# Attention pairs 2 and 3 are transposed by the DMA engine, and the later pairs follow another plan

## The chip, the cores and the metric

The kernel runs on one core of a Trainium2 chip. The metric is device time in microseconds (us) of one execution, taken as the median of several runs. The engines are TensorE (PE in the rows, with PEld for its weight loads), VectorE (DVE), ScalarE (ACT), GpSimd (POOL) and SyncE (SP), which here only issues DMAs. Each works through its own list of instructions in order, and waits on the others through semaphores.

## The reference

```python
def _attn_ref(q, k, v):                       # 8 batches, 8 heads, 576 tokens, 64 per head
    q_c = q.reshape(B, H, nc, chunk, D)       # chunk = 64; k_c and v_c alike
    scores = scale * np.matmul(q_c, k_c.transpose(0, 1, 2, 4, 3))
    scores = scores - np.max(scores, axis=-1, keepdims=True)
    attn = np.exp(scores)
    attn = attn / (np.sum(attn, axis=-1, keepdims=True) + 1e-09)
    return np.matmul(attn, v_c)

def _moe_ref(x, w_in, w_out):                 # x is 4608 x 512, d_ff is 2048
    h = x @ w_in
    sp = np.where(h > 20.0, h, np.log1p(np.exp(np.minimum(h, 20.0))))
    return ((h * np.tanh(sp)) @ w_out).astype(np.float32)
```

The output of the attention, with heads side by side, is the x of the second function.

## The kernel before

The 4608 tokens are 36 tiles of 128, taken as 18 pairs numbered 0 to 17. For each pair the attention goes through the same steps: scores on PE, maximum, subtraction, exponential on ScalarE, sums, reciprocal and normalisation on VectorE, a transposition of the normalised p, and then the values on PE (av), which end in x. The feed-forward part needs x.

**First part.** Pairs 0 to 3 feed two plain blocks of 16 slots each. In slot s PE does `up(s+1)` (12 matmuls into h), then any attention of the slot, then `down(s-1)` (12 matmuls into o_o). `down(i)` begins with g_lo(i), which VectorE makes at line 411 after ScalarE's g_hi(i). In the first block the fp32 weights are also prepared on the fly: SP loads a piece into `sums` (line 163), ScalarE does `scale` and `hi`, VectorE `bits` (lines 192 and 193) and `lo` (line 211). The table `softmax` says in which slot each step of pairs 2 and 3 stands. There the transposition is 8 PE matmuls with an identity (`a_transpose`, line 332) and a ScalarE copy out of PSUM (`a_copy`, line 342).

**Second part.** From then on a list of steps, about 1.2 us of PE each, alternates matmuls into al, b and g (line 881) with matmuls into d (line 1000). `MEET` gives the step at which each of the pairs 8 to 17 begins and ends; a pair of 14 steps uses the plan `NEAR`, one below 30 steps `MID`, a longer one `FAR`. Pairs of 28 steps or more already go through the DMA: for each half t of a pair GpSimd's `p_split` (line 787) parts the 16-bit halves of the words, `p_turn` (line 793, on SP) transposes them by DMA, and GpSimd's `p_join` (line 799) puts the words together again. The two halves share one spare room, so the second half runs seven steps behind. All other pairs are transposed by PE (line 770). Loads of q and k stand 9 steps ahead of a pair's start.

Every load and store but a few at the start is issued by SP, in the order of the program: an instruction there that waits holds back all that stand behind it.

Of the kernel before, what the change touches and what calls it, by code (L numbers as in the profile page):

```python
# [9 lines left out]
F32 = mybir.dt.float32  # L10
# [3 lines left out]
U16 = mybir.dt.uint16  # L14
# [4 lines left out]
P = 128  # L19
CHUNK = 64  # L20
# [5 lines left out]
def kernel(  # L26
# [65 lines left out]
    def view(name, start, shape, dtype=F32):  # L92

        n = math.prod(shape)
        o = rooms[name]
        assert start % 4 == 0 and start // 4 + n <= o.shape[1]
        o = o[:, start // 4 : start // 4 + n]
        if dtype != F32:
            o = o.bitcast(dtype)
        if len(shape) > 1:  # L100
            names = "abcde"[: len(shape)]
            o = o.rearrange(
                f"p ({' '.join(names)}) -> p {' '.join(names)}", **dict(zip(names, shape))
            )
        return o
# [232 lines left out]
    def a_copy(j, t=BOTH):  # L338
        d = st[j]
        if t.start == 0:  # L340
            d["ps"] = at.tile([P, 2, H, CHUNK], F32, name=f"ps_{j}", tag="A")
        nc.scalar.copy(
            out=d["ps"][:, t].rearrange("p t h k -> p (t h k)"),
            in_=d["pt", t.start][:, : t.stop - t.start].rearrange("p t g n -> p (t g n)"),
        )

    def a_values(j, t=BOTH, place=HOME):
        small_mm(banks(j, "av", t, place), st[j]["v"], st[j]["ps"], t)
# [431 lines left out]
            in_=d["pt"][:, t].rearrange("p g n -> p (g n)"),  # L780
        )

    def half_words(slot):
        return view("c", 2 * KB * slot, [DM]).bitcast(U16)

    def p_split(j, t):
        nc.gpsimd.tensor_copy(
            out=half_words((2, 0)[t]).rearrange("p (b n) -> p b n", b=2),
            in_=half_words(t).rearrange("p (n b) -> p b n", b=2),
        )  # L790

    def p_turn(j, t):
        nc.sync.dma_start_transpose(
            out=half_words(t).rearrange("p (m n) -> p m n", n=P), in_=half_words((2, 0)[t])
        )

    def p_join(j, t):
        st[j]["p", t] = view("c", 2 * KB * (2, 0)[t], [NG, 2, CHUNK])
        nc.gpsimd.tensor_copy(
            out=half_words((2, 0)[t]).rearrange("p (n b) -> p b n", b=2),  # L800
            in_=half_words(t).rearrange("p (b n) -> p b n", b=2),
        )

# [234 lines left out]
    def s_store(b, half, js):  # L1038
# [16 lines left out]
        "exp": {7: (2, 3)},  # L1055
        "sum": {7: (2,), 8: (3,)},
        "norm": {8: (2,), 9: (3,)},
        "t": {9: (2,), 12: (3,)},
        "v": {10: (2,), 13: (3,)},
    }  # L1060

    AHEAD = list(range(FIRST_TILE // 2, FIRST_TILE // 2 + 4))
# [19 lines left out]
    def slot(s):  # L1082
# [6 lines left out]
            up(s + 1, last="w")  # L1089
        if "v" in e:  # L1090
            a_values(e["v"])
        for j in a["t"]:
            a_transpose(j)
        for j in a["v"]:
            a_values(j)
        if 1 <= s < N - 1:
            down(s - 1)
        for j in a["s"]:
# [30 lines left out]
            a_transpose(e["norm"])  # L1129
        for j in a["norm"]:  # L1130
            a_norm(j)
        for j in a["t"]:
            a_copy(j)
        if s < NF and a["exp"]:
            g_hi(s)
            g_lo(s)
# [26 lines left out]
            a_copy(e["norm"])  # L1163
        for j in a["v32"]:
            load_v(j)
        later = quick.get(s + 1, {})
        if "load" in later and s > NF:
            e_load(later["load"], "k")
# [57 lines left out]
        for k, m in (2, 0), (5, 3), (3, 4), (4, 7):  # L1226
            when(z, m, lambda k=k: x_sum(b, k))

    MEET = (36, 50, 64, 92, 148, 162, 190, 204, 260, 288, 307)
    NEAR = dict(exp=5, sum=(6, 7), norm=(7, 8), t=11)  # L1230
    MID = dict(exp=5, sum=(8, 9), norm=(10, 12), t=16)
    FAR = dict(exp=33, sum=(36, 37), norm=(38, 40), t=44)
    pe = {}

    def plan_pair(j, start, end):

        n = NEAR if end - start < 16 else MID if end - start < 30 else FAR

        def at_(m, *ops):
            when(*divmod(m, STEPS), *ops)  # L1240

        def on_pe(m, op):
            pe.setdefault(divmod(m, STEPS), []).append(op)

        at_(8 if start == MEET[0] else start - 9, lambda: p_load(j))
        on_pe(start, lambda: p_scores(j, start // STEPS))
        at_(start + 3, lambda: load_v(j))
        for t in range(2):
            at_(start + 1 + 2 * t, lambda t=t: p_max(j, t))
            at_(start + 2 + 2 * t, lambda t=t: p_sub(j, t))  # L1250
            at_(start + n["exp"], lambda t=t: p_exp(j, t))
            at_(start + n["sum"][t], lambda t=t: p_sum(j, t))
            at_(start + n["norm"][t], lambda t=t: p_norm(j, t))
            if end - start < 28:
                at_(start + n["t"] + 1, lambda t=t: p_copy(j, t))
            else:
                m = start + n["norm"][0] + 7 * t
                at_(m + 1, lambda t=t: p_split(j, t))
                at_(m + 2, lambda t=t: p_turn(j, t))
                at_(m + 8, lambda t=t: p_join(j, t))  # L1260
            at_(end + 1, lambda t=t: a_x(j, t))
        if end - start < 28:
            on_pe(start + n["t"], lambda: p_transpose(j))
        on_pe(end, lambda: p_values(j))

# [19 lines left out]

    with tc.manual_schedule():
        prologue()
        x1_open()
        for s in range(N - 1):
            slot(s)  # L1290
            if s == N - 5:
# [32 lines left out]
        ps_b = ctx.enter_context(tc.tile_pool(name="ps_b", bufs=1, space=bass.MemoryType.PSUM))  # L1324
        for n in "b", "g":
            places[n] = ps_b.tile([P, DM], F32, name=n, tag=n)
        for j, pair in zip(range(AHEAD[-1] + 1, NPAIR), zip(MEET, MEET[1:])):
            plan_pair(j, *pair)
        for m, step in (5, t_sum), (6, t_diff), (21, t_hi), (23, t_lo):
            when(*divmod(m, STEPS), lambda step=step: step(*LAST_JOB))  # L1330
        for z in 3, 17:
# [52 lines left out]
```

## Time and profile before

| | before |
|---|---|
| median of 3 runs | 795.29 us (794.58 to 795.43) |
| the profiled execution | 795.96 us, of which 794.1 us is the span of its instructions |
| PE busy | 781.3 us, 98% of the span |
| DVE, ACT, POOL busy | 592.6, 475.9 and 296.1 us |
| granted TensorE clock | 0.999 on average |
| DMA | 204.95 MB, 258 GB/s |

The span runs from the first to the last instruction. "Busy" counts instructions that are running, so PE's 98% leaves some 13 us in which it stands still, half of them at the end.

### The profile page before, as it was taken

The page shows a single profiled execution, that of the slowest core. Times are in us where ns is not written, and L with a number is a line of the kernel's source. Part 1 is how long each engine was busy: PE and PEld are TensorE (multiplying, and loading weights), DVE is VectorE, ACT ScalarE, POOL GpSimd, SP SyncE. Part 2 cuts the span into 40 slices and gives each one's busy share as a digit, 9 for nine tenths or more (in the row PEclk, how much of TensorE's full clock was granted, in tenths as well). Part 3 has the DMA queues.
Part 4 walks back from the last instruction along what each step waited for, and adds up shares of the span by engine and source line. Part 5 has one row for each costly group of instructions (what it writes and reads, how often), then busy time and mean ns, then how long its engine had stood idle before and what let it go on. Part 6 is the DMA issues. An engine that isn't in the chain of part 4 may idle for free.

```text
span 794.1 us, 15299 instructions
## 1 busy us (share of the span) xinstructions
PE 781.3 (98%) x5940; PEld 701.4 (88%) x5940; DVE 592.6 (75%) x929; ACT 475.9 (60%) x855; POOL 296.1 (37%) x259
## 2 busy tenths in 40 slices
PE   8999999999999999999999999999999999999996
PEld 7887888888889999999899999999999999999986
DVE  6897978888866776799577679977575897455666
ACT  5988865666676665555566466647465654644440
POOL 2000026556363235533434435454433452333340
PEclk9999999999999999999999999999999999999999
DMA  7798867989978777765987866689965667866537
GB/s 292 245 312 292 276 229 242 350 285 333 374 244 295 268 263 222 291 225 181 328 333 237 297 254 233 220 234 373 284 235 185 227 217 242 291 224 220 182 117 172
DMA packets 95112, 204.95 MB, mean 258 GB/s; under 512 B 24128, under 2 KB 47168, under 8 KB 87872
## 3 DMA queue, kind: packets, MB, share of 16 engines
q1 hardware_dynamic: 90752, 202.01, 74.9%
q10 hardware_dynamic: 4288, 1.97, 1.0%
q8 instruction: 47, 0.77, 0.4%
q14 instruction: 25, 0.20, 0.1%
HBM read 162.53 MB, written 38.80 MB: 254 GB/s over the span
## 4 chain that ended last, share of the span: by engine, by line
PE 75%; DVE 10%; ACT 6%; DMA 3%; issue 2%; POOL 1%; SPq 0%; DVEq 0%; POOLq 0%; ACTq 0%
PE d L1000 28%; PE al L881 16%; PE o_o L424 8%; PE g L881 8%; PE h L389 7%; PE b L881 4%; DMA k<-in_k 2%; PE av L256 2%; DVE sums L1028 1%; DVE sums L1031 1%; PE al L720 1%; DMA v<-in_v 1%; DVE c L192 1%; PE s L256 1%; DVE c L760 1%
## 5 line engine op out<-in xcount | busy, mean ns | idle before, releaser
L1000 PE MATMUL d<-u,wo 128*128 128x448 f32 x796 | 203.8, 363 | 0.0
L1028 DVE TENSOR_TENSOR sums<-d,sums 128x448 f32<-128x448 f32 x192 | 118.8, 619 | 78.4 <-PE d L1000 78.1
L881 PE MATMUL al<-xo,ring 128*128 128x448 f32 x768 | 174.6, 362 | 0.0
L1000 PEld LDWEIGHTS d<-u,wo 128*128 128x128 f32 x796 | 148.6, 187 | 11.7 <-DVE u L960 0.6
L881 PEld LDWEIGHTS al<-xo,ring 128*128 128x128 f32 x768 | 143.3, 187 | 11.0 <-ACT sums L926 0.5
L881 PE MATMUL g<-xo,ring 128*128 128x448 f32 x384 | 87.6, 363 | 0.2 <-ACT y L926 0.2
L881 PEld LDWEIGHTS g<-xo,ring 128*128 128x128 f32 x384 | 71.6, 187 | 5.4 <-ACT y L926 0.6
L1000 PE MATMUL d<-yr,wo 128*128 128x448 f32 x192 | 56.7, 363 | 0.0
L1000 PE MATMUL d<-xo,wo 128*128 128x448 f32 x182 | 54.9, 364 | 0.0
L1000 PE MATMUL d<-g,wo 128*128 128x448 f32 x174 | 51.9, 363 | 0.2 <-DVE sums L1028 0.2
L950 ACT ACTIVATE b<-b 128x448 f32<-128x448 f32 x32 | 16.9, 528 | 52.0 <-DVE b L936 51.9
L640 POOL TENSOR_TENSOR c<-c 128x256 f32<-128x256 f32 x12 | 10.8, 901 | 98.2 <-DVE c L608 96.2
L881 PE MATMUL b<-xo,ring 128*128 128x448 f32 x192 | 43.6, 362 | 0.0
L950 ACT ACTIVATE y<-y 128x448 f32<-128x448 f32 x22 | 12.7, 577 | 47.6 <-DVE y L936 47.6
L982 POOL TENSOR_TENSOR z<-y,z 128x448 f32<-128x448 f32 x24 | 27.8, 1157 | 35.8 <-DVE y L982 21.9
L424 PE MATMUL o_o<-xo,g 128*128 128x512 f32 x168 | 40.8, 392 | 0.1
L389 PE MATMUL h<-x,xo 128*128 128x512 f32 x168 | 40.9, 392 | 0.0
L950 ACT ACTIVATE z<-g 128x448 f32<-128x448 f32 x32 | 17.4, 544 | 39.0 <-DVE g L936 28.0
L1000 PEld LDWEIGHTS d<-yr,wo 128*128 128x128 f32 x192 | 36.0, 187 | 2.7 <-ACT sums L1026 0.3
L881 PEld LDWEIGHTS b<-xo,ring 128*128 128x128 f32 x192 | 36.0, 187 | 2.5
L424 PEld LDWEIGHTS o_o<-xo,g 128*128 128x128 f32 x168 | 31.2, 188 | 6.6 <-DVE g L411 0.2
L389 PEld LDWEIGHTS h<-x,xo 128*128 128x128 f32 x168 | 31.2, 188 | 6.5
(261 smaller groups left out, 1656.3 us busy)
## 6 DMA issues: line engine op xcount, KB each, us to landing
ring<-dwi SPq DMA_DIRECT2D x56, 1024.0 KB, 7.1
wo<-dwo SPq DMA_DIRECT2D x112, 512.0 KB, 4.5
sums<-in_w_in SPq DMA_DIRECT2D x16, 512.0 KB, 5.4
sums<-in_w_out SPq DMA_DIRECT2D x16, 512.0 KB, 5.6
q<-in_q SPq DMA_DIRECT2D x16, 512.0 KB, 6.4
k<-in_k SPq DMA_DIRECT2D x16, 512.0 KB, 6.9
v<-in_v SPq DMA_DIRECT2D x16, 512.0 KB, 6.3
dwo<-sums SPq DMA_DIRECT2D x15, 512.0 KB, 5.2
```

What stands on the lines that cost most here:

```text
L192: nc.vector.scalar_tensor_tensor(out=c, in0=c, scalar=3, in1=a[:, :, 0], op0=left, op1=either)
L256: nc.tensor.matmul(o[h * CHUNK : (h + 1) * CHUNK, c, t - ts.start, g], lhsT=l[rows, t, 2 * g + h], rhs=r[rows, t, 2 * g + h], start=True, ...
L389: nc.tensor.matmul(h[:, cols], lhsT=wi(f, w_, kt), rhs=x[:, kt, cols], start=(n == 0), stop=(n == 3 * NK - 1),)
L424: nc.tensor.matmul(acc[t], lhsT=g[:, sl], rhs=w_part(f, w_), start=(f == 0 and n == 0), stop=(f == NF - 1 and n == 2),)
L640: nc.gpsimd.tensor_tensor(out=o, in0=a, in1=b, op=op)
L720: nc.tensor.matmul(d["s", c][h * CHUNK : (h + 1) * CHUNK, t, g], lhsT=d["q"][rows, t, 2 * g + h], rhs=d["k"][rows, t, 2 * g + h], start=Tr ...
L760: nc.vector.tensor_tensor(out=p, in0=p, in1=r.unsqueeze(3).broadcast_to([P, 2, NG, CHUNK]), op=ALU.mult)
L881: nc.tensor.matmul(o[:, :HALF], lhsT=w_[:, wn, kt * P : (kt + 1) * P], rhs=x[:, xn, kt], start=(n == 0 and k < 3), stop=(n == 5), skip_gro ...
L950: nc.scalar.activation(out=take(z, 12) if n == 12 else i, in_=i, func=AF.Mish)
L982: engine.tensor_tensor(out=o, in0=l, in1=r, op=ALU.subtract)
L1000: nc.tensor.matmul(o[:, :HALF], lhsT=wos[(len(DOWN) * y + kk) % 4][:, i, part, h * P : (h + 1) * P], rhs=x, start=(m == 0 and k in (5, 2, 1)),
L1028: nc.vector.tensor_tensor(out=o, in0=i, in1=o, op=ALU.add)
```

## The change

Pairs 2 and 3 no longer use PE and ScalarE for the transposition. GpSimd splits, SP issues the DMA transposes, GpSimd joins (`a_split`, `a_turn`, `a_join`), with the room `early` as the spare place for pair 2 and a fresh buffer for pair 3; `x1` is therefore opened later. The values of pair 2 stand in slot 11 where they were in slot 10. In the second part the two halves get separate spare rooms (the second one at the end of `x32`), the second half's split stands 2 steps behind the first's, each join 10 steps behind its normalisation, loads have a list of their own (`LOAD`), and pair 17 ends at step 316 and so goes through the DMA as well.

```diff
--- before.py
+++ after.py
@@ -343,6 +343,35 @@
             out=d["ps"][:, t].rearrange("p t h k -> p (t h k)"),
             in_=d["pt", t.start][:, : t.stop - t.start].rearrange("p t g n -> p (t g n)"),
         )
+
+    def words(x, t):
+        return x[:, t].bitcast(U16)
+
+    def a_split(j, x):
+        d = st[j]
+        d["x"] = x
+        d["w"] = d["p"].rearrange("p t g c k -> p t (g c k)")
+        for t in range(2):
+            nc.gpsimd.tensor_copy(
+                out=words(x, t).rearrange("p (b n) -> p b n", b=2),
+                in_=words(d["w"], t).rearrange("p (n b) -> p b n", b=2),
+            )
+
+    def a_turn(j):
+        d = st[j]
+        for t in range(2):
+            nc.sync.dma_start_transpose(
+                out=words(d["w"], t).rearrange("p (m n) -> p m n", n=P), in_=words(d["x"], t)
+            )
+
+    def a_join(j):
+        d = st[j]
+        for t in range(2):
+            nc.gpsimd.tensor_copy(
+                out=words(d["x"], t).rearrange("p (n b) -> p b n", b=2),
+                in_=words(d["w"], t).rearrange("p (b n) -> p b n", b=2),
+            )
+        d["ps"] = d["x"].rearrange("p t (h k) -> p t h k", k=CHUNK)
 
     def a_values(j, t=BOTH, place=HOME):
         small_mm(banks(j, "av", t, place), st[j]["v"], st[j]["ps"], t)
@@ -780,24 +809,27 @@
             in_=d["pt"][:, t].rearrange("p g n -> p (g n)"),
         )
 
-    def half_words(slot):
-        return view("c", 2 * KB * slot, [DM]).bitcast(U16)
+    def p_place(n):
+        return ("c", 2 * KB * n) if n < 3 else ("x32", 14 * KB)
+
+    def half_words(n):
+        return view(*p_place(n), [DM]).bitcast(U16)
 
     def p_split(j, t):
         nc.gpsimd.tensor_copy(
-            out=half_words((2, 0)[t]).rearrange("p (b n) -> p b n", b=2),
+            out=half_words(t + 2).rearrange("p (b n) -> p b n", b=2),
             in_=half_words(t).rearrange("p (n b) -> p b n", b=2),
         )
 
     def p_turn(j, t):
         nc.sync.dma_start_transpose(
-            out=half_words(t).rearrange("p (m n) -> p m n", n=P), in_=half_words((2, 0)[t])
+            out=half_words(t).rearrange("p (m n) -> p m n", n=P), in_=half_words(t + 2)
         )
 
     def p_join(j, t):
-        st[j]["p", t] = view("c", 2 * KB * (2, 0)[t], [NG, 2, CHUNK])
+        st[j]["p", t] = view(*p_place(t + 2), [NG, 2, CHUNK])
         nc.gpsimd.tensor_copy(
-            out=half_words((2, 0)[t]).rearrange("p (n b) -> p b n", b=2),
+            out=half_words(t + 2).rearrange("p (n b) -> p b n", b=2),
             in_=half_words(t).rearrange("p (b n) -> p b n", b=2),
         )
 
@@ -1055,8 +1087,10 @@
         "exp": {7: (2, 3)},
         "sum": {7: (2,), 8: (3,)},
         "norm": {8: (2,), 9: (3,)},
-        "t": {9: (2,), 12: (3,)},
-        "v": {10: (2,), 13: (3,)},
+        "split": {8: (2,), 9: (3,)},
+        "turn": {8: (2,), 10: (3,)},
+        "join": {9: (2,), 11: (3,)},
+        "v": {11: (2,), 13: (3,)},
     }
 
     AHEAD = list(range(FIRST_TILE // 2, FIRST_TILE // 2 + 4))
@@ -1089,10 +1123,10 @@
             up(s + 1, last="w")
         if "v" in e:
             a_values(e["v"])
-        for j in a["t"]:
-            a_transpose(j)
         for j in a["v"]:
             a_values(j)
+            if j == 2:
+                x1_open()
         if 1 <= s < N - 1:
             down(s - 1)
         for j in a["s"]:
@@ -1129,8 +1163,13 @@
             a_transpose(e["norm"])
         for j in a["norm"]:
             a_norm(j)
-        for j in a["t"]:
-            a_copy(j)
+        for j in a["join"]:
+            a_join(j)
+        for j in a["split"]:
+            if j == 2:
+                a_split(j, view("early", 0, [2, DM]))
+            else:
+                a_split(j, at.tile([P, 2, DM], F32, name=f"x_{j}", tag="A"))
         if s < NF and a["exp"]:
             g_hi(s)
             g_lo(s)
@@ -1163,6 +1202,8 @@
             a_copy(e["norm"])
         for j in a["v32"]:
             load_v(j)
+        for j in a["turn"]:
+            a_turn(j)
         later = quick.get(s + 1, {})
         if "load" in later and s > NF:
             e_load(later["load"], "k")
@@ -1226,13 +1267,14 @@
         for k, m in (2, 0), (5, 3), (3, 4), (4, 7):
             when(z, m, lambda k=k: x_sum(b, k))
 
-    MEET = (36, 50, 64, 92, 148, 162, 190, 204, 260, 288, 307)
+    MEET = (36, 50, 64, 92, 148, 162, 190, 204, 260, 288, 316)
+    LOAD = (8, 38, 52, 80, 118, 150, 178, 192, 230, 276)
     NEAR = dict(exp=5, sum=(6, 7), norm=(7, 8), t=11)
-    MID = dict(exp=5, sum=(8, 9), norm=(10, 12), t=16)
-    FAR = dict(exp=33, sum=(36, 37), norm=(38, 40), t=44)
+    MID = dict(exp=5, sum=(8, 9), norm=(10, 12))
+    FAR = dict(exp=33, sum=(36, 37), norm=(38, 40))
     pe = {}
 
-    def plan_pair(j, start, end):
+    def plan_pair(j, load, start, end):
 
         n = NEAR if end - start < 16 else MID if end - start < 30 else FAR
 
@@ -1242,7 +1284,7 @@
         def on_pe(m, op):
             pe.setdefault(divmod(m, STEPS), []).append(op)
 
-        at_(8 if start == MEET[0] else start - 9, lambda: p_load(j))
+        at_(load, lambda: p_load(j))
         on_pe(start, lambda: p_scores(j, start // STEPS))
         at_(start + 3, lambda: load_v(j))
         for t in range(2):
@@ -1251,15 +1293,15 @@
             at_(start + n["exp"], lambda t=t: p_exp(j, t))
             at_(start + n["sum"][t], lambda t=t: p_sum(j, t))
             at_(start + n["norm"][t], lambda t=t: p_norm(j, t))
-            if end - start < 28:
+            if n is NEAR:
                 at_(start + n["t"] + 1, lambda t=t: p_copy(j, t))
             else:
-                m = start + n["norm"][0] + 7 * t
+                m = start + n["norm"][t]
                 at_(m + 1, lambda t=t: p_split(j, t))
                 at_(m + 2, lambda t=t: p_turn(j, t))
-                at_(m + 8, lambda t=t: p_join(j, t))
+                at_(m + 10, lambda t=t: p_join(j, t))
             at_(end + 1, lambda t=t: a_x(j, t))
-        if end - start < 28:
+        if n is NEAR:
             on_pe(start + n["t"], lambda: p_transpose(j))
         on_pe(end, lambda: p_values(j))
 
@@ -1285,7 +1327,6 @@
 
     with tc.manual_schedule():
         prologue()
-        x1_open()
         for s in range(N - 1):
             slot(s)
             if s == N - 5:
@@ -1324,8 +1365,8 @@
         ps_b = ctx.enter_context(tc.tile_pool(name="ps_b", bufs=1, space=bass.MemoryType.PSUM))
         for n in "b", "g":
             places[n] = ps_b.tile([P, DM], F32, name=n, tag=n)
-        for j, pair in zip(range(AHEAD[-1] + 1, NPAIR), zip(MEET, MEET[1:])):
-            plan_pair(j, *pair)
+        for j, steps in zip(range(AHEAD[-1] + 1, NPAIR), zip(LOAD, MEET, MEET[1:])):
+            plan_pair(j, *steps)
         for m, step in (5, t_sum), (6, t_diff), (21, t_hi), (23, t_lo):
             when(*divmod(m, STEPS), lambda step=step: step(*LAST_JOB))
         for z in 3, 17:
```

On PE, the first block from slot 9 on, before the change. Here h is `up`, o_o is `down`, pt the transposition and av the values:

```order
L389 MATMUL h_920<-x_89,xo 128x512 x12
L332 MATMUL pt_0_933<-ident,p_643 128x128 x8
L424 MATMUL o_o_489<-xo,g 128x512 x6
L424 MATMUL o_o_490<-xo,g 128x512 x6
L389 MATMUL h_977<-x_89,xo 128x512 x12
L256 MATMUL av_0_990<-ps_962,v_814 64x64 x32
L424 MATMUL o_o_489<-xo,g 128x512 x6
L424 MATMUL o_o_490<-xo,g 128x512 x6
L389 MATMUL h_1056<-x_89,u 128x512 x12
```

The same slots with the change:

```order
L418 MATMUL h_919<-x_89,xo 128x512 x12
L453 MATMUL o_o_484<-xo,g 128x512 x6
L453 MATMUL o_o_485<-xo,g 128x512 x6
L418 MATMUL h_970<-x_89,xo 128x512 x12
L453 MATMUL o_o_484<-xo,g 128x512 x6
L453 MATMUL o_o_485<-xo,g 128x512 x6
L418 MATMUL h_1016<-x_89,u 128x512 x12
L256 MATMUL av_0_1029<-early,v_809 64x64 x32
```

The eight transposes are gone from slot 9, and the values of pair 2 have moved behind the `up` of slot 11.

On GpSimd, the end of the start-up and what follows it (p_638 is the p of pair 2, p_807 that of pair 3, L669 is line 640 of before, the first work on the second block's weights):

```order
L211 TENSOR_TENSOR ring<-c,ring 128x512 x2
L355 COPY early<-p_638 128x1024 x2
L370 COPY early<-p_638 128x2x512 x2
L355 COPY x_954<-p_807 128x1024 x2
L370 COPY x_954<-p_807 128x2x512 x2
L669 TENSOR_TENSOR c<-c 128x256 x2
```

Before, the row of line 640 came right behind that of line 211: the eight copies in slots 8 to 11 are new, and GpSimd had nothing there.

On SP's queue, slots 8 and 9 with the change (lines 163 load weights, lines 619 write prepared weights back to memory):

```order
L163 DMA sums<-in_w_out 128x1024
L163 DMA sums<-in_w_in 128x1024
L363 DMA_TRANSPOSE p_638<-early 128x8x128 x2
L619 DMA dwi_103<-wo 128x2x256 x2
L619 DMA dwo_115<-wo 128x2x256
L163 DMA sums<-in_w_out 128x1024
```

Without the row of line 363 these rows are those of before: the two transposes of pair 2 stand in front of three write-backs and the first weight load of slot 9.

## Rows read from the trace of the kernel before

**Rows 1.** Busy time by stretch: PE, PEld, DVE, ACT, POOL, then granted clock, DMA share, GB/s.
```profile
71.00:88.00 17.00, 15.83 (x133) 12.74 (x132) 16.65 (x26) 13.39 (x23) 0.00 (x0) 1.00 0.70 215
...
130.00:212.00 82.00, 82.00 (x724) 67.20 (x723) 65.75 (x86) 48.55 (x74) 46.98 (x49) 1.00 0.96 330
```

**Rows 2.** Timeline, PE, slots 9 to 12: start, us, instructions [idle before].
```profile
72.50 2.88 PE L389 MATMUL h<-x,xo 128*128 128x512 f32 x12
...
76.50 1.06 PE L332 MATMUL pt<-ident,p 128*128 128x128 f32 x8 [1.12 <-DVE p L323]
...
77.32 3.00 PE L424 MATMUL o_o<-xo,g 128*128 128x512 f32 x12
...
82.97 1.16 PE L256 MATMUL av<-ps,v 64*64 64x64 f32 x64
...
84.18 3.02 PE L424 MATMUL o_o<-xo,g 128*128 128x512 f32 x12
...
95.20 1.03 PE L332 MATMUL pt<-ident,p 128*128 128x128 f32 x8
...
95.99 2.98 PE L424 MATMUL o_o<-xo,g 128*128 128x512 f32 x12
```

**Rows 3.** Timeline, VectorE, slots 8 to 10.
```profile
76.27 0.68 DVE L411 TENSOR_TENSOR g<-z,g 128x512 fp32r<-128x512 f32 x1
...
78.80 1.22 DVE L310 TENSOR_REDUCE r<-p 128x16 f32<-128x1024 f32 x1
...
83.44 0.68 DVE L411 TENSOR_TENSOR g<-z,g 128x512 fp32r<-128x512 f32 x1
...
88.78 0.69 DVE L411 TENSOR_TENSOR g<-z,g 128x512 fp32r<-128x512 f32 x1 [0.79 <-ACT g L406]
```

**Rows 4.** GpSimd's groups of the join (L799) and split (L787) copies: busy us, mean ns.
```profile
L799 POOL COPY c<-c 128x1024 uint16<-128x1024 uint16 x10 | 14.7, 1469 | 0.4 <-DMA c<-c 0.3
...
L787 POOL COPY c<-c 128x1024 uint16<-128x1024 uint16 x10 | 10.8, 1084 | 4.4 <-PE d L1000 2.8 <-DVE c L760 1.2
```

**Rows 5.** Timeline, GpSimd and VectorE beside each other in block 2.
```profile
310.02 1.35 POOL L799 COPY c<-c 128x1024 uint16<-128x1024 uint16 x1
...
310.63 1.16 DVE L960 TENSOR_TENSOR g<-y,u 128x448 fp32r<-128x448 f32 x1
...
311.72 0.61 DVE L960 TENSOR_TENSOR g<-al,u 128x448 fp32r<-128x448 f32 x1
```

**Rows 6.** Source line of the DMA transpose: issue in ns, min/median/max, and time to landing.
```profile
L793 SPq DMA_TRANSPOSE c<-c x10: 1238/1282/2019, 302.2 to 565.9; - x10
...
DMA to landing us min/median/max: 3.0/3.4/7.2
```

**Rows 7.** A weight load: in the page's list (KB, us to landing), its issue, its use.
```profile
sums<-in_w_out SPq DMA_DIRECT2D x16, 512.0 KB, 5.6
...
78.35 0.34 SPq L163 DMA_DIRECT2D sums<-in_w_out  x1
...
86.09 0.68 ACT L170 ACTIVATE c<-sums 128x512 f32<-128x512 f32 x1
```

**Rows 8.** Waits of PE for k loads (us, times, longest), and such a load's issue.
```profile
PE al L720 <- DMA k<-in_k: 1.0, 2, 0.8
...
386.54 0.48 SPq L707 DMA_DIRECT2D k<-in_k  x1
```

**Rows 9.** Timeline, PE's weight loads behind a ScalarE copy to sums.
```profile
534.80 0.19 PEld L1000 LDWEIGHTS d<-yr,wo 128*128 128x128 f32 x1 [0.28 <-ACT sums L1026]
```

**Rows 10.** Timeline, PE, transposes of pair 17 between two groups of matmuls.
```profile
595.08 1.03 PE L770 MATMUL pt<-ident,c 128*128 128x128 f32 x8
...
595.87 0.45 PE L1000 MATMUL d<-g,wo 128*128 128x448 f32 x1
```

**Rows 11.** Busy time by stretch around the last matmul.
```profile
786.00:788.00 2.00, 1.75 (x9) 1.30 (x7) 1.93 (x5) 0.00 (x0) 0.00 (x0) 1.00 1.00 201
...
792.00:794.00 2.00, 0.00 (x0) 0.00 (x0) 0.00 (x0) 0.00 (x0) 0.00 (x0) 0.77 0.27 57
```

## The prediction

> **What bounds the kernel now.** I read the busy time by stretch first. Between 130 and 212 us PE is busy for all 82.00 us [rows 1]; nothing but PE's own work sets the time there, and a PE microsecond lost or saved earlier stays lost or saved to the end. The place where this does not hold is the stretch of the change, 71 to 88 us: PE is busy for 15.83 of 17.00 us, VectorE for 16.65 [rows 1]. So VectorE, not PE, is the bound in slots 8 and 9. The timelines show how. PE's `up` of slot 9 starts at 72.50, the transposes of pair 2 at 76.50 after a wait of 1.12 for VectorE's normalisation, and `down(8)` at 77.32 [rows 2]. On VectorE g_lo(8), which `down(8)` needs, follows the normalisation and runs from 76.27 to 76.95 [rows 3]. One slot later g_lo(9) ends at 83.44 + 0.68 = 84.12 [rows 3], and `down(9)` starts at 84.18 [rows 2]: that is a tie, PE could not have started earlier.
>
> **Step 1: the transposes of pairs 2 and 3 leave PE.** What they cost is 75.22 (72.50 plus 2.72 for twelve matmuls) to 77.32 for pair 2, 2.1 us with the wait, and 95.99 - 95.20 = 0.8 plus 0.1 that the next group takes longer, 0.9 for pair 3 [rows 2]. But `down(8)` still needs g_lo(8) at 76.95, so slot 9 gains only some 0.27 (start at 77.05). PE is then through `down(8)` and `up(11)` at 77.05 + 2 x 2.75 = 82.55 (2.75 is a quarter of the four groups between 84.18 and 95.20 [rows 2]) and stands until g_lo(9) at 84.12. That the values of pair 2 (84.18 - 82.97 = 1.2 [rows 2]) have left slot 10 gives nothing there, and they are paid in slot 11. Behind that point: before, `down(11)` starts 95.99 - 84.18 = 11.8 after `down(9)`; now 0.9 less for pair 3 and 1.2 more for the moved values, 12.1. Without anything else `down(11)` starts at 84.2 + 12.1 = 96.3, which is **+0.3**. The saving on PE is eaten whole by the wait for g_lo(9). The next g_lo is no bound there: g_lo(10) ends at 89.47 after a wait of 0.79 for ScalarE [rows 3], which copied pair 2's values to x just ahead and now does so a slot later (88.7 without it), and `down(10)` is now due at 84.2 + 6.7 = 90.9.
>
> **Step 2: eight copies on GpSimd, next to a full VectorE.** GpSimd was idle in this stretch (0.00 in [rows 1]). A split takes 1.08 us in the mean, a join 1.47 [rows 4]. Does VectorE feel them? The nearest row is a join from 310.02 to 311.37. VectorE's g<-y,u, two operands in SBUF, runs from 310.63 for 1.16, where its neighbour of the same line with an operand in PSUM takes 0.61 [rows 5]. It lost 0.55 and could begin only at 311.79 - 0.61 = 311.18, 0.19 before the join's end. So a copy can hold such an operation back for up to its duration less 0.19: 0.9 for a split, 1.3 for a join. VectorE's operations between g_lo(8) and g_lo(9) (`bits`, `lo`, the normalisation of pair 3) have both operands in SBUF; the sum over p at 78.80 (1.22 us [rows 3]) has one.
>
> The Trainium skill says it more strictly (SBUF — State Buffer, section "SBUF: two separate sides"): the port pair that VectorE and GpSimd share is an exclusive lock, held for the whole instruction, also against a VectorE operation with two SBUF inputs. The row agrees that VectorE is held, with 0.19 less than the whole. By the rule, an estimate, two splits and two joins cost 5.1 at most, and the sum below would be +3.3 instead of +2.2.
>
> Now the order. Both splits of pair 2 stand right behind the normalisation, in front of `bits`: 2 x 0.9 = 1.8. The transposes follow each split by an issue of 1.3 and land 3.4 after it, at most 7.2 [rows 6]: about 81.4 and 83.0. The first join falls on the sum over p (then 80.6 to 81.8) and costs 0.4 to 1.3, the second 1.3: 3.5 to 4.4, less if a gap is met. The ends for g_lo(9) are 1.8 (both joins land later) and 4.4; I take **3.7**, since the row is the same copy on the same engine and VectorE has no gap to give. PE then stands from 82.55 to 84.2 + 3.7 = 87.9 in one piece. The splits of pair 3 come behind g_lo(9) and push g_lo(10) to about 88.7 + 3.7 + 1.8 = 94.2, with `down(10)` due at 87.9 + 6.7 = 94.6: covered by 0.4. The joins of pair 3 can push g_lo(11): 0 to 1, I take **0.3**.
>
> **Step 3: SP's queue.** The two transposes stand in front of a weight load issued at 78.35 that ScalarE uses at 86.09 [rows 7]. They wait for the second split (about 79.6), issue for 2 x 1.3, then come three write-backs (an estimate from the 0.34 and 0.48 of the issues in [rows 7, 8]: 0.4 each, 1.2): the load leaves at 83.4, 5.0 late, and lands 5.6 later [rows 7], at 89.0. With VectorE late by step 2, ScalarE's `scale` comes only at about 90, so I cost it at nothing. Without step 2 the cover is gone: ScalarE is then some 2 us late, which g_lo(10)'s 2.2 us of slack just takes.
>
> **Step 4: the second part.** Pair 17 loses its transposes: 595.87 - 595.08 = 0.8, and 0.1 behind it: -0.9 [rows 10]. PE waits 1.0 in two places for k [rows 8]; one of these loads is issued at 386.54, on SP behind the second transpose of pair 11. `LOAD` puts the loads of pairs 12 and 16 21 steps earlier, ahead of the transposes: -1.0. At 534.80 PE's weights wait 0.28 for a ScalarE copy into `sums` [rows 9] that waits for a store queued late on SP; with the transposes nearer together the store leaves earlier: -0.2. Pair 17's four copies I cost at nothing: in the second stretch of rows 1 GpSimd is busy for 46.98 us and VectorE for 65.75 of 82.00, and PE never waits. Together **-2.1**; the other end is -0.9, if new waits of SP replace those removed.
>
> **The sum.** +0.3 + 3.7 + 0.3 - 2.1 = +2.2 us against the profiled execution's 795.96 us, 798.2. That execution lies 0.7 above the median of the runs, 795.29, so the forecast is **797.5 us**.
>
> **Rivals.**
> A. *GpSimd costs VectorE nothing* (the operations of this block take turns without loss). For it: most of block 2's VectorE operations next to a copy show nothing, but they read PSUM. Then +0.3 - 2.1 = -1.8: 793.5, on the other side of no change. It decides at a loss per copy under about 0.45 us, half of what rows 5 give.
> B. *It does what it seems to be for*: PE gets back 2.1 - 0.2 and 0.9, -2.8, and -2.1 later: 790.4. This needs VectorE to finish g_lo(9) some 1.6 earlier than in rows 3, and nothing in the diff takes work off VectorE ahead of it.
> C. *The clock falls in PE's gap.* The last matmul ends at about 787.8, and the granted clock is 1.00 until 792 and 0.77 in the mean of 792 to 794 [rows 11]: full for 1.1 us of these and then at half, so it fell 5.3 us after the matmul. PE's gap of step 2 is 87.9 - 82.55 = 5.3 too. No row shows how long it stays at 1.2 GHz instead of 2.4; nothing is the one bound, and if it lasts as long as the fall took, 5.3 us at half speed lose 2.7: 800.2.
> D. *Early and late cancel*: the joins of pair 2 land behind g_lo(9), step 2 costs 2, and the sum is about +0.5: 795.8.
>
> **How the numbers follow.** Forecast (796 to 798.8 with the bounds of step 2) 0.45, C 0.12, A 0.17, B 0.08, D 0.18. I call 0.2%, 1.6 us, the least that such a measurement can tell from no change, so "slower" begins at 796.9. Of the forecast some 0.37 lies above it, C all, a little of D: 0.52. A lies on the lower border (793.7) and gives 0.09 to faster and 0.08 to no change; B is faster; D and the rest of the forecast are no change: faster 0.18, same 0.30, slower 0.52. The range from 793.4 to 800.0 leaves out B and half of C. The likeliest case's own range is 796.0 to 798.8.
>
> **What would show it.** Right: one long idle time of PE in slot 10, put down to VectorE's g_lo, `bits` and `lo` at 1.2 to 2 us instead of 0.69 beside the copies, `down(11)` at about 100 instead of 95.99; and from there PE without a wait, the waits for k gone, no PE transposes of pair 17. Wrong: VectorE's operations keep 0.69 beside the copies (A), `down(9)` starts before 84 (B), a granted clock under 1 near 88 us (C), or the time until 130 us is unchanged and the gain in the second part is other than 2.1.

## The result, and the profile after

The changed kernel takes 800.74 us (median of 4 runs, 800.0 to 800.97), the kernel before 795.36 beside it: a ratio of 1.0059, 95% interval 1.0041 to 1.0077. That is 4.7 us by the ratio (5.4 between the two medians): slower, clear of the noise, by far less than 2%. The forecast was 797.5, and the range ended at 800.0. The profiled execution took 800.97 us, its span 799.2: 5.1 more than before's.

The busy time in the stretch of the change, columns as in [rows 1]:

```profile
71.00:88.00 17.00, 10.63 (x45) 8.21 (x44) 16.76 (x21) 10.06 (x18) 6.38 (x5) 0.95 0.69 180
```

VectorE is as full as before in slots 8 and 9 (the time in which an operation is held counts as busy), GpSimd now works beside it, and PE has 5.2 us less of busy time (15.83 before), of which some 2 are pair 2's transposes and values, which have left this stretch. Where PE stands is on its timeline, against [rows 2]:

```profile
76.94 3.01 PE L453 MATMUL o_o<-xo,g 128*128 128x512 f32 x12 [1.45 <-DVE g L440]
79.80 2.88 PE L418 MATMUL h<-x,xo 128*128 128x512 f32 x12
87.59 5.49 PE L453 MATMUL o_o<-xo,g 128*128 128x512 f32 x12 [4.92 <-DVE g L440]
92.88 3.09 PE L418 MATMUL h<-x,u 128*128 128x512 f32 x12
95.90 1.16 PE L256 MATMUL av<-early,v 64*64 64x64 f32 x64
...
102.57 2.88 PE L453 MATMUL o_o<-xo,g 128*128 128x512 f32 x12
...
108.10 1.16 PE L256 MATMUL av<-x,v 64*64 64x64 f32 x64
```

Two things show here. `down(9)` starts at 87.59 instead of 84.18, after one wait of 4.92 us for g_lo(9) (now L440). And it takes 5.3 us to its successor instead of 2.85. `down(11)` starts at 102.57 instead of 95.99, 6.6 later. VectorE and GpSimd beside each other, against [rows 3]:

```profile
76.21 0.68 DVE L440 TENSOR_TENSOR g<-z,g 128x512 fp32r<-128x512 f32 x1
76.81 1.52 DVE L192 SCALAR_TENSOR_TENSOR c<-c,sums 128x512 uint32<-128x512 uint32 x1
78.37 1.41 DVE L193 SCALAR_TENSOR_TENSOR c<-sums,c 128x512 uint32<-128x512 uint32 x1
...
81.54 1.16 DVE L315 TENSOR_SCALAR r<-r 128x16 f32<-128x16 f32 x1
...
83.58 1.63 DVE L193 SCALAR_TENSOR_TENSOR c<-sums,c 128x512 uint32<-128x512 uint32 x1
...
86.86 0.68 DVE L440 TENSOR_TENSOR g<-z,g 128x512 fp32r<-128x512 f32 x1
```
```profile
76.52 2.71 POOL L355 COPY early<-p 128x1024 uint16<-128x1024 uint16 x2 [53.98 <-ACT sums L179]
81.31 1.36 POOL L370 COPY early<-p 128x1024 uint16<-128x1024 uint16 x1 [2.08 <-DMA p<-early]
83.22 1.49 POOL L370 COPY early<-p 128x1024 uint16<-128x1024 uint16 x1 [0.55 <-DMA p<-early]
```

Each of the four lengthened VectorE operations lies beside a copy. Against 0.69 (0.18 for the small one) they lose 0.83, 0.72, 0.98 and 0.94, together 3.47, and g_lo(9) ends 3.42 later than in [rows 3]. The small operation at 81.54 ends at 82.70, 0.03 after the join. The sum over p, which ran from 80.30 and lay under the start of that join, kept its 1.21.

The granted clock (the eighth column) around the long `down(9)`:

```profile
84.00:86.00 2.00, 0.00 (x0) 0.00 (x0) 2.00 (x3) 0.76 (x2) 0.71 (x1) 1.00 1.02 269
86.00:88.00 2.00, 0.41 (x1) 0.41 (x2) 2.00 (x3) 1.06 (x2) 0.82 (x1) 0.61 1.02 244
88.00:90.00 2.00, 2.00 (x6) 1.52 (x6) 1.97 (x2) 0.00 (x0) 1.89 (x2) 0.50 1.03 363
90.00:92.00 2.00, 2.00 (x6) 1.55 (x5) 1.97 (x4) 1.54 (x3) 0.00 (x0) 0.50 0.76 200
92.00:94.00 2.00, 2.00 (x8) 1.57 (x7) 2.00 (x4) 2.00 (x5) 0.00 (x0) 0.69 0.95 262
94.00:96.00 2.00, 2.00 (x13) 1.40 (x15) 1.97 (x4) 2.00 (x4) 0.00 (x0) 1.00 0.71 203
```

PE goes from 2.4 to 1.2 GHz while it stands, near 86.4 (0.61 is full speed for 0.4 of the 2 us), 3.8 us after its last matmul ended at 82.68, and is back near 93.2. It worked at half speed from 87.59 to 93.2, 5.6 us, and so lost 2.8.

SP's queue, against [rows 7], and PE's waits of the second part, against [rows 8, 9]:

```profile
77.81 3.45 SPq L363 DMA_TRANSPOSE p<-early  x2
...
83.07 0.43 SPq L163 DMA_DIRECT2D sums<-in_w_out  x1
```
```profile
92.86 4.40 SPq L363 DMA_TRANSPOSE p<-x  x2
97.30 1.09 SPq L619 DMA_DIRECT2D dwi<-xo  x2
98.50 1.06 SPq L163 DMA_DIRECT2D sums<-in_w_out  x2
99.65 0.46 SPq L246 DMA_DIRECT2D v<-in_v  x1
```
```profile
PE o_o L453 <- DVE g L440: 6.4, 2, 4.9
PE d L1032 <- ACT sums L1058: 0.5, 1, 0.5
```

The waits for k are gone, those for ScalarE's copies to `sums` are 0.5. Pair 3's transposes hold SP for 4.40 us, and the weight loads and the load of pair 3's values, av(3), stand behind them. PE's list shows no wait for that load, but it is close:

```profile
L246 SPq DMA_DIRECT2D v<-in_v x1: 455/455/455, 99.6 to 99.6; - x1
...
DMA to landing us min/median/max: 8.2/8.2/8.2
```

Issued at 99.65, it lands near 107.9, and av(3) starts at 108.10. PE's own late chain and this second chain, over SP's queue, end within 0.3 us of each other.

### The profile page after: what moved, and what is told of

It is laid out like the page before. It is cut to its first block, busy times and chain, and to the rows that moved or that the text cites. A ratio compares the mean times of both kernels' runs of the same rounds, so it can differ in the third digit from the quotient of the medians.

```text
span 799.2 us, 15293 instructions
## 1 busy us (share of the span) xinstructions
PE 781.2 (98%) x5916; PEld 700.4 (88%) x5916; DVE 598.0 (75%) x929; ACT 473.0 (59%) x851; POOL 315.2 (39%) x271
## 4 chain that ended last, share of the span: by engine, by line
PE 79%; DVE 10%; ACT 5%; DMA 4%; issue 2%; SPq 0%; DVEq 0%; ACTq 0%
PE d L1032 30%; PE al L913 17%; PE g L913 9%; PE o_o L453 8%; PE h L418 7%; PE b L913 4%; PE av L256 2%; DMA q<-in_q 1%; DVE sums L1060 1%; DVE sums L1063 1%; DVE c L192 1%; PE al L749 1%; DMA sums<-in_w_out 1%; DVE c L193 1%; DMA sums<-in_w_in 1%
## 5 line engine op out<-in xcount | busy, mean ns | idle before, releaser
L453 PE MATMUL o_o<-xo,g 128*128 128x512 f32 x168 | 43.4, 410 | 6.4 <-DVE g L440 6.4
L453 PEld LDWEIGHTS o_o<-xo,g 128*128 128x128 f32 x168 | 32.9, 198 | 14.2 <-DVE g L440 7.2
L1032 PEld LDWEIGHTS d<-xo,wo 128*128 128x128 f32 x182 | 34.0, 187 | 3.3 <-ACT sums L1058 0.9
```

The lines of the kernel that those rows point to most:

```text
L453: nc.tensor.matmul(acc[t], lhsT=g[:, sl], rhs=w_part(f, w_), start=(f == 0 and n == 0), stop=(f == NF - 1 and n == 2),)
L1032: nc.tensor.matmul(o[:, :HALF], lhsT=wos[(len(DOWN) * y + kk) % 4][:, i, part, h * P : (h + 1) * P], rhs=x, start=(m == 0 and k in (5, 2, 1)),
```

## The experiments

Absolute times in two executions differ by up to 2 us at g_lo(8) already (it starts at 76.27 before and at 75.03 to 77.20 below), so I compare distances within a trace, and times through the ratio to runs of the kernel before on the same chip. A trace is of one execution; where that one is far from the median of its kernel, I say so.

**1. The two parts apart.** The table of pairs 2 and 3 alone, and the plan of pairs 8 to 17 alone.

```diff
early_only:  "t"/"v" of pairs 2, 3 -> "split", "turn", "join", "v"
late_only:   LOAD, MEET ... 316, NEAR/MID/FAR, p_place
```


> Only pairs 2 and 3 by DMA, later pairs as before. Theory: the whole loss is made here, 6.6 us: 802.0, and a clock that falls near 86 us. Rival: the two parts need each other (the shifted loads meet the first block's work) and this alone costs under 4: below 799.5.


Measured: 802.77 us, ratio 1.0083 (1.0069 to 1.0097). The first part makes a loss at least as large as the whole change's. In its trace PE is 5.4 us behind the kernel before at the end of the first part; another 1.0 comes near 545 us, where PE waits for k and for copies to `sums` under the old plan of the later pairs. The first block is that of the changed kernel, but here the clock was at half for 3.4 us instead of 6.8, and av(3) then follows the landing of its load:

```profile
87.05 4.54 PE L453 MATMUL o_o<-xo,g 128*128 128x512 f32 x12 [4.70 <-DVE g L440]
...
106.68 1.16 PE L256 MATMUL av<-x,v 64*64 64x64 f32 x64
```
```profile
99.36 0.41 SPq L246 DMA_DIRECT2D v<-in_v  x1
...
DMA to landing us min/median/max: 7.2/7.2/7.2
```

The load lands near 106.6. av(3) starts 19.7 us after the end of g_lo(9), against 20.6 in the changed kernel: by these two traces, an estimate, about 1 us of the 2.8 that the clock costs there could come back before the second chain holds PE.

> Only the new plan of pairs 8 to 17, with the first block as before. Theory: the later pairs alone gain 1.5 us (down(11) starts 6.6 later with the whole change, the end only 5.1), so 793.9. Rival 1, the first block's loss is not carried whole to the end and the later plan gives nothing: 795.4. Rival 2, my forecast's size for this part: 793.3.


Measured: 795.32 us, ratio 0.9994 (0.9985 to 1.0004), the time of rival 1. PE's waits for k are gone, but a new one has come:

```profile
PE d L1032 <- ACT sums L1058: 1.4, 2, 0.8
```

**2. The copies without the transposes.** Four copies of pair 2's size in slot 8 that nobody reads; pairs 2 and 3 stay on PE.

```diff
+ if s == 8: for t in range(2): nc.gpsimd.tensor_copy(out=half[t] ..., in_=p2[:, t] ...)
+            for t in range(2): nc.gpsimd.tensor_copy(out=half[t + 2] ..., in_=half[t] ...)
```


> The kernel before, with its PE transposes and no DMA transposes, plus four GpSimd copies of pair 2's shape in slot 8 whose result nobody reads. Theory, the copies hold VectorE: bits take 1.4 to 1.6 us instead of 0.69 beside them, g_lo(9) ends 3.4 late, down(9) starts at 87.6 instead of 84.18, and with a gap of 3.5 the clock stays: 798.8. Rival, the DMA transposes and SP's queue do the harm: VectorE keeps its durations, 795.4.


Measured: 799.76 us, ratio 1.0045 (1.0029 to 1.0061). No DMA transpose is issued in the first block here, and VectorE's operations stretch as in the change:

```profile
75.96 1.52 DVE L192 SCALAR_TENSOR_TENSOR c<-c,sums 128x512 uint32<-128x512 uint32 x1
77.52 1.41 DVE L193 SCALAR_TENSOR_TENSOR c<-sums,c 128x512 uint32<-128x512 uint32 x1
78.85 1.78 DVE L211 TENSOR_TENSOR xo<-c,xo 128x512 fp32r<-128x512 f32 x1
80.56 1.21 DVE L310 TENSOR_REDUCE r<-p 128x16 f32<-128x1024 f32 x1
```
```profile
75.67 2.71 POOL L1139 COPY early<-p 128x1024 uint16<-128x1024 uint16 x2 [53.39 <-ACT sums L179]
78.33 3.53 POOL L1144 COPY early<-early 128x1024 uint16<-128x1024 uint16 x2
```

Three operations lose 0.83, 0.72 and 1.09, 2.64 in all. The fourth copy lies beside the sum over p, which has one operand in SBUF and loses nothing (1.21). The clock adds to the loss: it falls here too, which the expectation did not have, around a wait of 1.91 (granted 0.52 from 86 to 88 us), and `down(9)` takes 4.59 instead of 3.02. So the copies hold VectorE by themselves, and rival A is out.

**3. The most that the first part could give.** Before, without the transposes of pairs 2 and 3 and the copies behind them.

```diff
- for j in a["t"]: a_transpose(j)
- for j in a["t"]: a_copy(j)
+ for j in a["t"]: st[j]["ps"] = st[j]["p"].rearrange("p t g c k -> p t (g c) k")
```


> The kernel before without the transposes of pairs 2 and 3 and without ScalarE's copies of them (the values are computed from the probabilities as they lie, so this part of the output is not the reference's): the most that the first-block part of the change could have given if the DMA path cost nothing. Theory (my first step: without pair 2's transposes TensorE only waits longer for g_lo(9), VectorE being full; pair 3's 0.8 us come back in full): 795.5 - 0.8 = 794.7 us, with a longer wait ahead of down(8) or down(9). Rival (TensorE is the bound there, both pairs' transposes come back): 795.5 - 1.9 = 793.6 us.


Measured: 796.76 us (12 runs, 794.6 to 799.7), ratio 1.0016 (1.0003 to 1.0029): nothing gained, where both theories had a gain of 0.8 us or more. The trace is of the slowest of the 12 executions (799.70). There PE waits in their stead, and works at 1.2 GHz afterwards:

```profile
77.94 4.61 PE L424 MATMUL o_o<-xo,g 128*128 128x512 f32 x12 [2.01 <-DVE g L411]
```

In this stretch the transposes cost nothing: they lay in PE's wait for VectorE. That they also kept its clock up there is shown by this one execution only. Rival B is out, for any way of transposing in this schedule.

**4. The clock held.** Spare matmuls of 128x128 in slot 10's gap of the changed kernel, first 24.

```diff
+ if s == 10:
+     for _ in range(24): nc.tensor.matmul(o[:, :P], lhsT=ident, rhs=ident, start=True, stop=True)
```


> The whole change, with 24 spare 128x128 matmuls on PE behind up(11) in slot 10, where PE stands still for 4.9 us. They are further work whose output nobody reads. Theory: the fall of the clock costs 2.8 us by itself, so 797.9 with a granted clock of 1.00 throughout and down(9) starting at the same 87.6. Rival: the clock only shows the wait and PE has slack behind it: 800.7.


Measured: 802.6 us, ratio 1.0083 (1.0068 to 1.0098). `down(9)` ran at full clock, and yet the end came later: PE then waited 2.12 us ahead of pair 3's values.

> The whole change with the spare matmuls of the run before (they keep TensorE busy in slot 10's gap), and in addition the two weight loads of slot 11 are issued on GpSimd's queue instead of SP's, where they stood behind the two transposes of pair 3. That run's chain says that the values of pair 3 waited 2.12 us because one of these loads was issued at 99.69 only, landed at 104.68, and ScalarE and VectorE needed it ahead of g_lo; and that the clock then fell once more (the down product after them took 4.50 us instead of 2.88). Theory (SP's queue is the next bound behind the gap): the wait goes to under 0.5 us, the down product takes 2.9 us at full clock, 802.6 - 2.1 - 1.6 = 798.9 us, 1.8 below the changed kernel's 800.7. Rival (the values wait for VectorE, which the joins hold, whatever SP does): the wait stays near 2 us and the time at 802.6.


Measured: 805.42 us, ratio 1.0123 (1.0108 to 1.0138): worse. Neither of the two runs is a clean test: with 24 spare matmuls the pool gave the load of pair 3's values a buffer that comes free with the joins only, and SP waited for that. With 18 the buffer is that of the changed kernel.

> The run with spare matmuls again, with 18 of them instead of 24. With 24 the pool gave the values' load of pair 3 another buffer, one that comes free only with the joins (SP waited 2.7 us for them), so that run and the one with the weight loads on GpSimd's queue had a wait that the changed kernel does not have; with 18 the buffer and its wait are those of the changed kernel. Theory A (the clock is what made the change dearer than forecast): 1.00 from 84 to 96 us, down(9) in 3.0 us, down(11) at 100.2, and the end 2.4 us earlier, 798.3 us. Theory B (behind the gap SP's queue is the next bound: the load of pair 3's values stands behind pair 3's transposes, is issued near 99.6 and lands near 107.8 in the changed kernel too, where the values start at 108.10): down(11) at 100.2 as well, but av(3) waits about 2 us, starts no earlier than 107, and the end stays near 800.5 us. B is the likelier.


Measured: 800.25 us, ratio 1.0065 (1.0053 to 1.0078): no gain over the changed kernel's 1.0059. The trace is of the slowest of the six executions (802.77; the others took 799.7 to 800.9). The clock stays at 1.00 in every stretch from 80 to 120 us, and PE stands later instead; what it waits for comes by SP's queue, and ScalarE waits there too:

```profile
88.30 3.06 PE L453 MATMUL o_o<-xo,g 128*128 128x512 f32 x12 [0.67 <-DVE g L440]
...
108.87 1.16 PE L256 MATMUL av<-x,v 64*64 64x64 f32 x64 [2.59 <-DMA v<-in_v]
```
```profile
93.56 5.02 SPq L363 DMA_TRANSPOSE p<-x  x2
98.64 1.90 SPq L619 DMA_DIRECT2D dwi<-xo  x2
100.65 0.89 SPq L163 DMA_DIRECT2D sums<-in_w_out  x2
101.63 0.40 SPq L246 DMA_DIRECT2D v<-in_v  x1
```
```profile
106.25 0.65 ACT L170 ACTIVATE c<-sums 128x512 f32<-128x512 f32 x1 [4.60 <-DMA sums<-in_w_out]
```

Theory B of this run holds: a second chain, over pair 3's transposes on SP's queue, ends where the slow clock ends. The 2.59 us are too much for its size, since in this execution the load leaves 13.4 us after the end of g_lo(9) and in the changed kernel's 12.1. The landing near 107.9 in the changed kernel's own trace, 0.2 ahead of av(3), shows the tie without that.

**5. The values' load first.** The same, with `load_v(3)` ahead of slot 11's weight loads.

```diff
+ if s == 11: load_v(3)
  w("load", n + 4)
```


> The 18 spare matmuls, and the load of pair 3's values put at the head of slot 11, ahead of that slot's two weight loads on SP's queue (it stays behind pair 3's two transposes, and waits for av(2), which ends near 95). Theory B (the load's landing sets av(3)): issued near 97.3 instead of 99.6, it lands 2 us earlier, av(3) starts near 106 and the end falls to 798.5 us. Rival (the weight loads, now 0.4 us later, or DMA traffic as a whole set av(3)): the wait ahead of av(3) or of the down product behind it stays near 2 us, 800.5 us.


Measured: 801.69 us, ratio 1.0077 (1.0065 to 1.0089). The values started without a wait at 105.06, but the weights became the bound: ScalarE waited 5.80 us for them, `down` behind the values waited 2.54 us for g_lo, and the clock fell there (it took 4.61). The rival's 2 us of waiting came, and the time is dearer than both theories.

```profile
106.28 0.66 ACT L170 ACTIVATE c<-sums 128x512 f32<-128x512 f32 x1 [5.80 <-DMA sums<-in_w_out]
```

In either order, something that stands behind the 5 us of transposes on SP comes late.

**6. Pair 3 alone, pair 2 alone.**

```diff
pair3_only:  "t": {9: (2,)}, "split": {9: (3,)}, "turn": {10: (3,)}, "join": {11: (3,)}
pair2_only:  "split": {8: (2,)}, "turn": {8: (2,)}, "join": {9: (2,)}, "t": {12: (3,)}
```


> The kernel before with pair 3 alone transposed by the DMA engine (split in slot 9, transposes in slot 10, join in slot 11, values in slot 13 as before); pair 2 stays on TensorE, later pairs as before. TensorE loses 0.8 us of transposes ahead of down(11). Theory A (only the copies beside slots 8 and 9's full VectorE cost something, and pair 3's fall where VectorE has slack): 795.5 - 0.8 = 794.7 us. Theory B (SP's queue: the transposes take some 4.5 us of it in slot 10, the weight loads of slot 11 come about 2.5 us later, and the values of pair 3 wait for them): a wait of about 2 us ahead of av(3) and perhaps a clock fall of 1.5 behind it, 796.7 to 798.2. After the run with the spare matmuls B is the likelier.


Measured: 799.32 us, ratio 1.0041 (1.0028 to 1.0053). Dearer than both theories: 3.3 us by the ratio. The copies of pair 3 hold VectorE as those of pair 2 do, twice, and PE waits 1.14 and 1.79 us for g_lo (before: no such wait in the slots behind `down(9)`). Theory B's wait ahead of av(3) is not there, and the clock stays at 1.00. In the trace 1.4 of the loss stand ahead of 112 us; the rest comes near 390 and 540 us, where PE waits 2.2 us for k and for copies to `sums` (1.0 before).

```profile
83.52 1.41 DVE L193 SCALAR_TENSOR_TENSOR c<-sums,c 128x512 uint32<-128x512 uint32 x1
84.85 1.52 DVE L211 TENSOR_TENSOR u<-c,u 128x512 fp32r<-128x512 f32 x1
...
92.78 1.65 DVE L192 SCALAR_TENSOR_TENSOR c<-c,sums 128x512 uint32<-128x512 uint32 x1
94.47 1.66 DVE L193 SCALAR_TENSOR_TENSOR c<-sums,c 128x512 uint32<-128x512 uint32 x1
```

> The kernel before with pair 2 alone transposed by the DMA engine (split and transposes in slot 8, joins in slot 9, values in slot 11); pair 3 on TensorE, later pairs as before. Theory A (two chains end at nearly the same time: TensorE's, with the gap ahead of down(9) and the lower clock behind it, and that of pair 3, with its transposes on SP's queue; either alone sets the end): the gap costs 0.3 + 3.4, the clock 2.9, 795.6 + 6.6 = 802.2 us at most, and less where before had slack behind, near 801. Theory B (pair 3's transposes on SP's queue alone set the end): the end falls to pair 2's gap alone, 799.3 us or less.


Measured: 803.21 us, ratio 1.0105 (1.0091 to 1.0120), more than the whole change. In the trace, of an execution of 804.69, `down(9)` starts 3.8 later than before and takes 2.1 too long; the moved values are 1.1, which here no transpose saved from pair 3 pays for (my 0.3 in this expectation forgot that). Theory B is out: pair 2's chain alone, with the gap and the clock behind it, is enough for the whole loss.

> Pair 2 alone by the DMA engine, with the 18 spare matmuls in slot 10's gap. Without pair 3's transposes on SP's queue there is nothing behind the gap to take the clock's gain away: clock 1.00 from 84 to 96 us, no wait over 0.5 us ahead of av(3), and 795.6 + 0.3 + 3.4 = 799.3 us, 2 to 3 us less than pair 2 alone without the spare matmuls. Rival (the clock is never worth its price, the time comes back at another wait): the same time as without them.


Measured: 801.94 us, ratio 1.0079 (1.0066 to 1.0091): 1.3 us less than without the spare matmuls, where 2 to 3 were expected, and the two intervals just meet. No wait for SP's queue is left behind the gap. The clock fell once more in this trace, around slot 8's wait of 1.94 us (`down(8)` took 4.61), which the spare matmuls do not fill. PE was late by that, and the spare matmuls ended 0.7 us behind g_lo(9) (89.01 against 88.27), which is part of what is missing.

**7. The second part.** Its two pieces alone, and the old spacing of the two transposes with the rest of it.

```diff
loads_only:                 + LOAD = (8, 38, 52, 80, 118, 150, 178, 192, 230, 276)
pair17_only:                - MEET = (..., 288, 307)   + MEET = (..., 288, 316)
late_spaced, after_spaced:  - m = start + n["norm"][t] + m = start + n["norm"][0] + 7 * t
                            - at_(m + 10, p_join ...)   + at_(m + 8, p_join ...)
```


> The kernel before with nothing changed but the steps at which q and k of pairs 8 to 17 are loaded (the changed kernel's list). By my fourth step the waits of TensorE for k, 1.0 us, go: 795.5 - 1.0 = 794.5 us. Rival (another wait takes their place, as in the run of the late part alone): 795.3 us.


Measured: 794.92 us, ratio 0.9987 (0.9976 to 0.9997), a gain of 1.0 us by the ratio. Its trace has no wait for k and none in its place: the theory holds.

> The kernel before with nothing changed but that pair 17 is transposed by the DMA engine, and its values computed at step 316 instead of 307. By my fourth step TensorE's 16 transposes go, 0.9 us: 795.5 - 0.9 = 794.6 us. Rival (they filled a wait that stays): 795.5 us. That the copies beside VectorE cost something: late there, where VectorE has slack, nothing.


Measured: 795.47 us, ratio 0.9997 (0.9988 to 1.0006), the rival's time. In its trace, of an execution of 793.95, PE does gain 0.9 us where the transposes were; the median does not show it.

> The new plan of pairs 8 to 17 alone, with the first block as before, and with the old spacing of a pair's two DMA transposes (seven steps apart, join eight steps after the norm) put back; loads moved and pair 17's transposes on the DMA engine stay. Theory (the two transposes, put two steps apart, stand ahead of the out stores on SP's queue, the stores land later, ScalarE's copies to sums wait for them and TensorE's d for the copies, 1.4 us in all): the wait goes to 0.3 us or less and the time from 795.3 to 794.2. Rival (the wait comes from TensorE being ahead, since k no longer holds it): the wait stays near 1.4 and the time at 795.3.


Measured: 794.45 us, ratio 0.9981 (0.9972 to 0.9990), faster than both kernels. But the theory is not shown by it: PE's wait is 1.0 instead of the expected 0.3, and ScalarE's copy at 388.55 waits as long for the store as without the spacing (3.40 there). Of the two waits without it, 0.83 at 389 us and 0.53 at 536, only the second is gone:

```profile
388.55 0.53 ACT L1058 COPY sums<-d 128x448 f32<-128x448 f32 x1 [3.55 <-DMA out<-sums]
```

> The changed kernel with the old spacing of a later pair's two DMA transposes (seven steps, join eight after the norm). The late part alone gained 0.9 us by it. Theory: the same here, 800.7 - 0.9 = 799.8 us. Rival: the changed kernel's waits for the stores are only 0.5 us in all, so 800.4 us.


Measured: 800.31 us, ratio 1.0059 (1.0047 to 1.0071), the changed kernel's ratio: the spacing gives it nothing that shows.

## Why the prediction was wrong

*The direction was right, and so was the first mechanism, GpSimd's copies holding VectorE. The size was not: two costs had been put at nothing or nearly so.* Up to pair 3's values the trace has +6.5 us (108.10 against 101.62 in the trace before), and I had +4.3 there; another 0.3 comes by 150 us, and the second part then gives back 1.6, where I had 2.1.

- **Step 1**, PE's saving is eaten by the wait for g_lo(9): right. Leaving the transposes out altogether gains nothing, not even the 0.8 that I had for pair 3.
- **Step 2**, 3.7 for the copies on VectorE: 3.42, with some luck in how it is made up. The splits cost 1.55 (1.8 forecast) and the joins 1.92, but the first join did not slow the sum over p, as I had it; it held the small operation behind it. The Trainium skill (SBUF — State Buffer, section "SBUF: two separate sides") has the lock last for the whole instruction, and the trace agrees to 0.2 us: the small operation takes 0.18 alone and ended 0.03 after the join, so it began 0.15 before the join's end, near the 0.19 of [rows 5]. The estimate of 5.1 is too much here, because each copy began while a VectorE operation was already running (g_lo(8) under the first split, the sum over p under the first join) and held only the next one. With 5.1 for 3.7 the sum is +3.6; the +3.3 in the prediction leaves out the 0.3 for pair 3.
- **The step that failed first is the clock, which the sum had at nothing.** "Nothing is the one bound" was a reading of one row, PE's clock after the very last matmul [rows 11], 5.3 us after it. In the gap it fell after 3.8 us, and rival C's 2.7 us (12% in my chances) came in full: 2.8. The row bounded nothing: other waits brought the clock down sooner (2.01 us in the run without transposes).
- **The joins of pair 3, 0.3, and step 3, nothing, failed too, though the total hides it.** For pair 2 step 3 was right: its weight load left at 83.07 (83.4 forecast) and cost nothing. But pair 3 alone costs 3.3 us. Its four copies hold VectorE for some 3.5, and its transposes hold SP for 3.1 to 5.0, where I had counted only those of pair 2. In the changed kernel this chain runs beside PE's slow stretch and ends with it (the load of the values lands near 107.9, av(3) starts at 108.10). That is why holding the clock gives no gain that shows (800.25 against 800.74). Among the changed kernel's own four runs, too, the one with the highest mean clock (0.997, the others 0.993 and 0.994) took 800.53, in the middle of the four.
- **Step 4**, -2.1: in the changed kernel's trace it came to -1.6. Near 390 us a wait of 0.49 for a copy to `sums` stands where 0.80 for k was (behind it PE is 0.14 us less late), between 500 and 540 us several waits of 0.3 or less went (-0.61), and pair 17's transposes went (-0.88). Alone, the second part gains 0.5 us by the ratio, at most a little more than 1 (0.9985 at the lower end), because the new wait is 1.4 there.

The sum as the trace has it: +0.3 + 3.4 + 2.8 + 0.3 - 1.6 = +5.2 on a span of 794.1, and 799.2 was measured. The 2.8 for the clock is what PE lost at half speed, not what a held clock would give back.

By the ratios the second part is worth 1.9 us beside the first one (1.0083 to 1.0059) and 0.5 alone. The intervals allow both to be about 1, but the traces, of one execution each, point the same way: with the first block late, the old plan loses another 1.0 near 545 us and the new one gains 1.6, while alone the new one gains 0.4. Left open: which piece makes the spaced version faster, since only the moved loads show a gain by themselves.

## What to carry to other kernels

Work taken off an engine is worth what the engine next in line allows: here PE's transposes filled its wait for VectorE, and every replacement that loads VectorE, even by copies on another engine, lands on the path. Price a new idle time of TensorE with the clock behind it (here a wait of 1.91 us already had a halved clock behind it), and look for the second chain before removing the first: here both ended within 0.3 us of each other. Transposes on a shared queue are charged to all that stands behind them.

## What the runs showed of the hardware

- GpSimd copies of 128x1024 uint16 lengthened VectorE operations on two SBUF operands beside them from 0.69 to 1.4 to 1.8 us, and one of a 128x16 tensor with a scalar from 0.18 to 1.16. A sum over 128x1024 with one SBUF operand kept its 1.21 beside such a copy (the run with four unread copies).
- TensorE's granted clock fell from 1.00 to 0.50 (2.4 to 1.2 GHz) around idle times of 1.91 (four unread copies), 1.94 (pair 2 alone with spare matmuls), 2.01 (no transposes) and 4.92 us (the change), and stayed full over 1.79 (pair 3 alone), 2.00 and 2.59 (the change with 18 spare matmuls). The 1.94 and the 2.00 stand in the same slot, behind the same list of matmuls: the length of one wait does not decide it.
- Once down, the clock stayed so for 6.8 us in the traces of the change and of pair 2 alone, and for 3.4 us in those of pairs 2 and 3 alone, of the unread copies and of the run without transposes.
- The two DMA transposes of a pair held SP's queue for 3.0 to 5.0 us, where the rows before had a median issue of 1.3 each.
